# A decoder block on one Trainium2 core: the last gate's weights as one load of 128 rows and one of twelve blocks of eight rows

## The chip, the core and the metric

The kernel runs on one core of a Trainium2 chip. The core has five engines that run their own instruction streams and meet at semaphores: TensorE (PE, matrix products into PSUM), VectorE (DVE), ScalarE (ACT), GpSimd (POOL) and SyncE (SP), which here issues nearly all loads. Loads from HBM into SBUF, whose 128 rows are called partitions, are carried out by 16 DMA engines that work side by side; a load counts as landed when every engine that takes part has finished its share. The metric is the device time of one execution in microseconds (us).

## The reference

It is one block of a transformer for four sequences with one new position each (B = 4, D = 512), with adaptive layer norm from a condition `c`. Cut to what matters:

```python
mod = (silu(c) @ w_mod).reshape(4, 6, 1, 512)
sa, ca, ga, sb, cb, gb = mod[:, 0], ..., mod[:, 5]
h = layernorm(x) * (1 + ca) + sa
x = x + ga * attention(h)          # 32 heads, 8 groups, the last 2048 of 8192 keys and values
h = layernorm(x) * (1 + cb) + sb
x = x + gb * ((silu(h @ w1) * (h @ w3)) @ w2)
```

`w_mod` has 512 rows and 6 x 512 columns. The last gate, `gb`, needs the 512 rows of its last 512 columns: 1 MB of float32.

## The kernel before

All of it is float32 and nearly all of it is loading: 101 MB of weights, keys and values pass through SBUF once. Two buffers, `KV0` and `KV1` (16384 columns of 128 partitions each), take turns for the keys and values of the eight head groups, and `WP` takes attention's projections.

The order of the loads is that of SyncE's instructions, lines 91 to 125, through the helper `load` (lines 88 and 89). Waits on semaphores hold a load back until the buffer that it overwrites is free; lines 95 to 116 are attention's. Behind attention come, in this order: `wm_in` (three of the modulations) and `f1_in` (`w1` and a part of `w3`) into `KV0`, lines 118 and 119; then, once the last group's values have been used, into `KV1`: `f2_in` (the rest of `w3`) in two parts (lines 121 and 122), `gb_in`, the weights of the last gate, on the semaphore `dgb` (line 123), and `w2_in` in six pieces with the semaphores `dw0` to `dw5`, cut at the chunks 0, 4, 8, 10, 12, 13 and 14 of 512 columns (lines 124 and 125, `W2_CUTS`).

At the start, `t0_in` (line 91) brings `c`, arranged as 128 partitions by 16 columns (4 blocks of 128 rows by 4 sequences), and the first two modulations' weights. ScalarE and VectorE make `sc = silu(c)` of it (lines 181 to 188); TensorE multiplies with it from line 312 on.

TensorE's stream has the block `pair` (lines 326 to 352), run four times for two head groups each, `query` and `leave`, and then the feed-forward part in one run. The end of it, which the change touches:

- lines 403 to 440: the products with `w1` and `w3`, silu and the hidden layer `hidT`;
- lines 443 to 446: TensorE waits for `dgb` and multiplies `sc` with the four blocks of 128 rows of the gate's weights. Each block k of four has its own four PSUM rows from 32k on in the bank `bM`;
- line 448: ScalarE copies the whole bank to `gb_sb`;
- lines 452 to 475: the product with `w2`, piece by piece as `dw0` to `dw5` arrive. Behind piece 0, TensorE adds the gate's four partial sums with the matrix `same` (lines 461 to 465), and ScalarE copies them to `gbJ`; behind piece 1, VectorE copies the first sums to `y_sb` (line 471), which TensorE adds behind piece 2 (line 475);
- lines 477 to 482: gate and residual on VectorE, and the store.

`_layout` (line 487) arranges the inputs on the host before the launch. The functions that the diff touches:

Of the kernel before, what the change touches and what calls it, by code (L numbers as in the profile page):

```python
# [5 lines left out]
AF = mybir.ActivationFunctionType  # L6
# [4 lines left out]
B, D, HQ, G, SK, DH, W, FF = 4, 512, 32, 8, 8192, 128, 2048, 1792  # L11
P = 128
# [2 lines left out]
EPS = 1e-5  # L15
CHUNKS = [(j, c) for c in range(4) for j in range(4) if c < 2 or j < 3]
HEAD = 8
W2_CUTS = [0, 4, 8, 10, 12, 13, 14]
PAIRS = G // 2

# [20 lines left out]
        return (self.sem, self.n)  # L41


def block_kernel(nc, x_in, t0_in, t1_in, kv_in, w_in, wm_in, f1_in, f2_in, gb_in, w2_in, out):
    T, v, s, gp, S = nc.tensor, nc.vector, nc.scalar, nc.gpsimd, nc.sync

    def sems(names):
        return [nc.alloc_semaphore(n) for n in names.split()]

    def sb(name, cols, rows=P):  # L50
        return nc.alloc_sbuf_tensor(name, (rows, cols), F32).ap()

    def bank(name):
        return nc.alloc_psum_tensor(name, (P, 512), F32).ap()

    (first,) = sems("first")
    A = Queue(nc, s, "act")
    V = Queue(nc, v, "dve")
    L = Queue(nc, gp, "pool")
    dx, dt0, dt1, dkv, dk, dva, dvb, dwo, dm, df1, df2a, df2b, dgb = sems("dx dt0 dt1 dkv dk dva dvb dwo dm df1 df2a df2b dgb")  # L60
    dw = sems(" ".join(f"dw{i}" for i in range(len(W2_CUTS) - 1)))
    z_ok, q_ok, p_ok, k_ok, va_ok, vb_ok, pt_ok, o_ok, ot_ok = sems("z_ok q_ok p_ok k_ok va_ok vb_ok pt_ok o_ok ot_ok")
# [2 lines left out]

    KV = [sb("KV0", 16384), sb("KV1", 16384)]
    WP = sb("WP", 8192)
    T0 = KV[1][:, : 16 + 4096]
    x_sb = sb("x_sb", 512, B)
    ident, same, eps = sb("ident", P), sb("same", B), sb("eps", 1)  # L70
    sc, e1, e2 = sb("sc", 16), sb("e1", 16), sb("e2", 16)
    hT, h2T = sb("hT", 16), sb("h2T", 16)
    Z = sb("Z", B * 28)
    q_sb, p_sb, o_sb, a_sb, y_sb, g_sb, u_sb, gb_sb = [sb(n, 512) for n in "q_sb p_sb o_sb a_sb y_sb g_sb u_sb gb_sb".split()]
# [10 lines left out]
    bS, bQ, bT, bP, bO, bX, bA, bM = [bank(n) for n in "bS bQ bT bP bO bX bA bM".split()]  # L85


    def load(dst, src, sem):
        S.dma_start(dst, src).then_inc(sem, 16)  # L89

    load(T0, t0_in, dt0)
    s.dma_start(WP[:, 4096:], t1_in).then_inc(dt1, 16)
# [27 lines left out]
    S.wait_ge(o_done, G)  # L120
    load(KV[1][:, :3072], f2_in[:, :3072], df2a)
    load(KV[1][:, 3072:6144], f2_in[:, 3072:], df2b)
    load(KV[1][:, 6144:8192], gb_in, dgb)
    for a, b, sem in zip(W2_CUTS[:-1], W2_CUTS[1:], dw):
        load(KV[1][:, 8192 + a * 512 : 8192 + b * 512], w2_in[:, a * 512 : b * 512], sem)


    l_eps = L.op(gp.memset(eps, EPS))
    t = L.op(gp.memset(ident, 0.0))
# [49 lines left out]
    v_same = V.op(v.tensor_reduce(same, ident.rearrange("p (j i) -> p i j", i=32)[:, :B, :], axis=AX.X, op=ALU.add))  # L179

    A.wait((dt0, 16))
    t = A.op(s.activation(e1, T0[:, :16], AF.Exp, scale=-1.0))
    V.wait(t)
    t = V.op(v.tensor_scalar(e2, e1, 1.0, None, op0=ALU.add))
    V.wait(t)
    t = V.op(v.reciprocal(e2, e2))
    V.wait(t, (dt0, 16))
    t_sc = V.op(v.tensor_mul(sc, T0[:, :16], e2))  # L188

    A.wait((pe, 1))  # L190
    t_sa = A.op(s.copy(sa_sb, bM[32 : 32 + B, :]))
# [1 line left out]
    t = V.op(v.scalar_tensor_tensor(xs, bM[:B, :], 1.0, xc, op0=ALU.add, op1=ALU.mult))  # L193
# [71 lines left out]
    def mm(o, lhsT, rhs, start=True, stop=True):  # L265
        return T.matmul(o, lhsT, rhs, start=start, stop=stop, skip_group_check=True)  # L266
# [45 lines left out]
    T.wait_ge(V.sem, t_sc[1])  # L312
    for k in range(4):
        for i in range(2):
            ins = mm(bM[32 * i : 32 * i + B, :], sc[:, k * B : (k + 1) * B], T0[:, 16 + (2 * k + i) * 512 : 16 + (2 * k + i + 1) * 512], k == 0, k == 3)
    ins.then_inc(pe, 1)
    T.wait_ge(V.sem, t_h[1])
    for k in range(4):
        ins = T.transpose(bT[:, k * B : (k + 1) * B], h[:, k * P : (k + 1) * P], ident[:B, :B])
# [51 lines left out]
    for k in range(4):  # L371
        for i in range(3):
            at = (3 * k + i) * 512
            ins = mm(bX[32 * i : 32 * i + B, :], sc[:, k * B : (k + 1) * B], KV[0][:, at : at + 512], k == 0, k == 3)
# [5 lines left out]
    t = V.op(v.tensor_mul(ag, bM[:B, :], ga_sb))  # L380
# [13 lines left out]
    for k in range(4):  # L394
        ins = T.transpose(bT[:, k * B : (k + 1) * B], h[:, k * P : (k + 1) * P], ident[:B, :B])
# [4 lines left out]
    def view(t_):  # L400
        return t_.rearrange("p (c j i) -> p c j i", c=4, j=4)
# [4 lines left out]
    for k in range(4):  # L406
        for j in range(4):
            at = 6144 + k * 2048 + j * 512
            ins = mm(bQ[32 * j : 32 * j + B, :], h2T[:, k * B : (k + 1) * B], KV[0][:, at : at + 512], k == 0, k == 3)
# [3 lines left out]
    for k in range(4):  # L413
# [5 lines left out]
        for j in range(3):  # L419
            at = k * 1536 + j * 512  # L420
            ins = mm(bA[32 * j : 32 * j + B, :], h2T[:, k * B : (k + 1) * B], KV[1][:, at : at + 512], k == 0, k == 3)
    ins.then_inc(pe, 1)
    A.wait((pe, 7))
    t = A.op(s.activation(view(eT), view(bP)[:, :, :, :B], AF.Exp, scale=-1.0))
    V.wait(t)
    t = V.op(v.tensor_scalar(dT, eT, 1.0, None, op0=ALU.add))
    V.wait(t)
    t = V.op(v.reciprocal(rT, dT))
# [7 lines left out]
    for c in range(4):  # L436
        ins = T.transpose(bS[:, c * P : c * P + 96], u_sb[:96, c * P : (c + 1) * P], ident[:96, :96])
# [2 lines left out]
    t_hid = V.op(v.tensor_mul(view(hidT)[:, :, :3], view(sT)[:, :, :3], view(bS)[:, :, :3, :B]))  # L440


    T.wait_ge(dgb, 16)
    for k in range(4):
        ins = mm(bM[32 * k : 32 * k + B, :], sc[:, k * B : (k + 1) * B], KV[1][:, 6144 + 512 * k : 6144 + 512 * (k + 1)])
    ins.then_inc(pe, 1)
    A.wait((pe, 10))
    t_gb = A.op(s.copy(gb_sb, bM))
    T.wait_ge(V.sem, t_hid[1])
    hw = view(hidT)  # L450
    w2 = KV[1][:, 8192 : 8192 + 14 * 512].rearrange("p (n m) -> p n m", n=14)
    for i in range(len(W2_CUTS) - 1):
        T.wait_ge(dw[i], 16)
        for n in range(W2_CUTS[i], W2_CUTS[i + 1]):
            jj, c = CHUNKS[n]
            if n < HEAD:
                ins = mm(bO[32 * (n % 4) : 32 * (n % 4) + B, :], hw[:, c, jj, :], w2[:, n, :], n < 4, n >= HEAD - 4)
                continue
            for j in range(4):
                ins = mm(bX[32 * j : 32 * j + B, :P], hw[:, c, jj, :], w2[:, n, j * P : (j + 1) * P], n == HEAD, n == 13)  # L460
        if i == 0:
            T.wait_ge(A.sem, t_gb[1])
            for j in range(4):
                ins = mm(bT[32 * j : 32 * j + B, :P], same, gb_sb[:, j * P : (j + 1) * P])
# [13 lines left out]
    t = V.op(v.tensor_mul(yt, bX[:, :P], gbJ))  # L478
# [8 lines left out]
def _layout(i):  # L487
    import numpy as np

    def a(t):  # L490
        return np.ascontiguousarray(t)

    k = i["A_k_cache"][:, :, SK - W :, :].reshape(B, G, NT, 512, DH)
    v = i["A_v_cache"][:, :, SK - W :, :].reshape(B, G, NT, 4, P, DH)
    k = k.transpose(1, 4, 2, 0, 3).reshape(G, P, 8192)
    v = v.transpose(1, 4, 2, 0, 3, 5).reshape(G, P, 8192)
    wm = i["w_mod"].reshape(4, P, 6, 512).transpose(1, 0, 2, 3)
    c = i["c"].reshape(B, 4, P).transpose(2, 1, 0).reshape(P, 16)
    wq = i["A_wq"].reshape(4, P, G, 512).transpose(2, 1, 0, 3).reshape(G, P, 2048)
    wo = i["A_wo"].reshape(G, R, P, D).transpose(0, 2, 1, 3).reshape(G, P, 2048)  # L500
    pairs = [[wo[2 * p], wo[2 * p + 1]] + ([wq[2 * p + 2], wq[2 * p + 3]] if p < 3 else [wo[6], wo[7]]) for p in range(4)]
    w1 = i["B_w1"].reshape(4, P, FF).transpose(1, 0, 2)
    w3 = i["B_w3"].reshape(4, P, FF).transpose(1, 0, 2)
    w2 = i["B_w2"].reshape(14, P, D)
    return {
        "x_in": a(i["A_x"].reshape(B, D)),
        "t0_in": np.concatenate([c, wm[:, :, 1::-1].reshape(P, 4096)], 1),
        "t1_in": np.concatenate([wq[0], wq[1]], 1),
        "kv_in": np.concatenate([k, v], 2),
        "w_in": np.stack([np.concatenate(p, 1) for p in pairs]),  # L510
        "wm_in": a(wm[:, :, 2:5]).reshape(P, 6144),
        "f1_in": np.concatenate([w1, w3[:, :, 1536:]], 2).reshape(P, 8192),
        "f2_in": a(w3[:, :, :1536]).reshape(P, 6144),
        "gb_in": a(wm[:, :, 5]).reshape(P, 2048),
        "w2_in": a(np.stack([w2[4 * j + c_] for j, c_ in CHUNKS], 1)).reshape(P, 14 * D),
    }

# [14 lines left out]
```

## Time and profile before

| | us |
|---|---|
| median of 3 runs | 243.03 (243.0 to 243.1) |
| the profiled execution | 243.09 |
| its span, first to last instruction | 241.7 |
| TensorE busy, matmuls | 137.8 (57% of the span) |
| VectorE busy | 38.6 (16%) |
| ScalarE busy | 25.1 (10%) |
| GpSimd busy | 1.7 (1%) |

The profile is of one execution. Its page gives each engine's busy time, the DMA queues, the chain of work that ended last and the costliest groups of instructions; further views of the same trace give windows of time, waits and single instructions. The 16 DMA engines serve several queues: q1 is SyncE's loads and q10 ScalarE's, while q8 and q14 carry the fetches of the engines' own instructions. The views give what all 16 engines move together, and no view says which engine moved a packet.

### The profile page before, as it was taken

The page shows a single profiled execution, that of the slowest core. Times are in us where ns is not written, and L with a number is a line of the kernel's source. Part 1 is how long each engine was busy: PE and PEld are TensorE (multiplying, and loading weights), DVE is VectorE, ACT ScalarE, POOL GpSimd, SP SyncE. Part 2 cuts the span into 40 slices and gives each one's busy share as a digit, 9 for nine tenths or more (in the row PEclk, how much of TensorE's full clock was granted, in tenths as well). Part 3 has the DMA queues.
Part 4 walks back from the last instruction along what each step waited for, and adds up shares of the span by engine and source line. Part 5 has one row for each costly group of instructions (what it writes and reads, how often), then busy time and mean ns, then how long its engine had stood idle before and what let it go on. Part 6 is the DMA issues. An engine that isn't in the chain of part 4 may idle for free. (4 is left out here: it accounts for less than half of the span.)

```text
span 241.7 us, 2238 instructions
## 1 busy us (share of the span) xinstructions
PE 137.8 (57%) x940; PEld 38.0 (16%) x940; DVE 38.6 (16%) x126; ACT 25.1 (10%) x54; POOL 1.7 (1%) x14
## 2 busy tenths in 40 slices
PE   3004677726771478267713782877137869656964
PEld 0000122201220013112200130121001312111211
DVE  3003203202200022022000220130002222133112
ACT  2002002100010011010100110011002100133110
POOL 2000000000000000000000000000000000000000
PEclk9999959968798579887985898679758997995999
DMA  7998989899989898999898989998989999999993
GB/s 266 440 511 358 510 361 499 369 423 439 504 369 499 369 499 370 423 428 504 369 499 369 499 369 423 434 510 369 499 347 445 442 396 445 449 431 394 413 415 116
DMA packets 4045, 101.34 MB, mean 419 GB/s; under 512 B 452, under 2 KB 580, under 8 KB 1096
## 3 DMA queue, kind: packets, MB, share of 16 engines
q1 hardware_dynamic: 3888, 99.17, 95.7%
q10 hardware_dynamic: 152, 2.11, 2.1%
q8 instruction: 3, 0.05, 0.1%
q14 instruction: 2, 0.02, 0.0%
HBM read 101.20 MB, written 0.07 MB: 419 GB/s over the span
## 5 line engine op out<-in xcount | busy, mean ns | idle before, releaser
L266 PE MATMUL bS<-KV,Z 128*16 128x512 f32 x256 | 42.7, 828 | 39.2 <-PEq L269 39.2
L266 PE MATMUL bO<-KV,pT 128*16 128x512 f32 x256 | 32.5, 652 | 0.5
L266 PEld LDWEIGHTS bS<-KV,Z 128*16 128x16 f32 x256 | 9.3, 123 | 67.1 <-issue 67.1
L222 DVE TENSOR_REDUCE MX<-bS 128x1 f32<-128x512 f32 x8 | 5.5, 692 | 80.4 <-PE bS L266 80.4
L266 PE MATMUL bM<-KV,sc 128*4 128x512 f32 x24 | 6.9, 801 | 16.6 <-DVE sc L188 16.6
L230 ACT ACTIVATE p_sb<-bS,NB 128x512 f32<-128x512 f32 x8 | 5.5, 687 | 101.2 <-DVE NB L228 101.2
L287 PE MATMUL bP<-ident,p_sb 128*128 128x128 f32 x32 | 5.6, 303 | 16.6 <-PEq L269 16.6
L266 PE MATMUL bA<-WP,oT 128*4 128x512 f32 x64 | 11.1, 773 | 4.3 <-PEq L269 4.3
L266 PEld LDWEIGHTS bO<-KV,pT 128*16 128x16 f32 x256 | 8.2, 107 | 23.9 <-issue 23.9
L251 ACT ACTIVATE o_sb<-bO,LB 128x512 f32<-128x512 f32 x8 | 5.5, 687 | 48.8 <-PE bO L266 48.8
L266 PE MATMUL bQ<-WP,hT 128*4 128x512 f32 x64 | 9.2, 647 | 0.6 <-DVE hT L197 0.6
L287 PE MATMUL bX<-ident,o_sb 128*128 128x128 f32 x32 | 5.0, 280 | 7.2 <-PEq L269 7.2
L254 DVE TENSOR_REDUCE oT<-bX 128x16 f32<-128x64 f32 x8 | 1.8, 224 | 43.6 <-PE bX L287 43.6
L287 PEld LDWEIGHTS bP<-ident,p_sb 128*128 128x128 f32 x32 | 3.6, 148 | 24.0 <-issue 24.0
L287 PE MATMUL bT<-ident,q_sb 128*128 128x128 f32 x32 | 5.5, 298 | 3.2 <-PEq L269 3.2
L201 ACT ACTIVATE q_sb<-bQ 128x512 f32<-128x512 f32 x8 | 4.7, 593 | 13.3 <-PE bQ L266 13.3
L287 PEld LDWEIGHTS bX<-ident,o_sb 128*128 128x128 f32 x32 | 3.4, 141 | 14.3 <-issue 14.3
L235 DVE COPY pT<-bP 128x256 f32<-128x256 f32 x8 | 3.4, 424 | 13.5 <-PE bP L287 13.5
L266 PE MATMUL bQ<-KV,h2T 128*4 128x512 f32 x32 | 5.3, 816 | 0.3 <-DVE h2T L398 0.3
L287 PEld LDWEIGHTS bT<-ident,q_sb 128*128 128x128 f32 x32 | 3.6, 150 | 8.0 <-issue 7.7
L266 PEld LDWEIGHTS bM<-KV,sc 128*4 128x4 f32 x24 | 1.0, 104 | 22.4 <-DVE sc L188 18.2
L266 PE MATMUL bX<-KV,sc 128*4 128x512 f32 x24 | 4.2, 592 | 0.0
(100 smaller groups left out, 65.2 us busy)
## 6 DMA issues: line engine op xcount, KB each, us to landing
WP<-w_in SPq DMA_DIRECT2D x3, 4096.0 KB, 22.0
KV<-kv_in SPq DMA_DIRECT2D x1, 4096.0 KB, 24.3
KV<-f_in SPq DMA_DIRECT2D x1, 4096.0 KB, 28.0
KV<-kv_in SPq DMA_DIRECT2D x1, 3072.0 KB, 31.1
KV<-wm_in SPq DMA_DIRECT2D x1, 3072.0 KB, 18.4
KV<-f_in SPq DMA_DIRECT2D x2, 1536.0 KB, 19.2
KV<-t_in SPq DMA_DIRECT2D x1, 2056.0 KB, 12.2
WP<-t_in ACTq DMA_DIRECT2D x1, 2048.0 KB, 12.4
```

What stands on the lines that cost most here:

```text
L201: A.op(s.mul(q_sb, bQ, DH**-0.5), q_ok)
L222: t = V.op(v.reduce_max(MX[:, 0:1], bS, axis=AX.X))
L230: A.op(s.activation(p_sb, bS, AF.Exp, bias=NB[:, 0:1], accum_out=SM[:, 0:1]), p_ok)
L235: v.tensor_copy(pT.rearrange("p (t b c r) -> p c b t r", t=NT, b=B, c=4), bP.rearrange("p (c b i) -> p c b i", c=4, b=B)[:, :, :, :16].rea ...
L251: A.op(s.mul(o_sb, bO, LB[:, 0:1]), o_ok)
L254: V.op(v.tensor_reduce(oT.rearrange("p (r b) -> p r b", r=R), diag, axis=AX.X, op=ALU.add), ot_ok)
L266: return T.matmul(o, lhsT, rhs, start=start, stop=stop, skip_group_check=True)
L287: ins = T.transpose(dst[:, c * P : (c + 1) * P], src[:, c * P : (c + 1) * P], ident)
```

## The change

Nothing of what is computed changes. The 512 columns of the gate's weights are cut at `GA = 320`. For the first 320 columns, the 512 rows are still four blocks of 128. For the other `GB = 192` columns, the first 128 rows are one block, and the other 384 rows are four blocks of 96.

- `gb_in` holds the 128-partition parts, 4 x 320 + 192 = 1472 columns for 2048. A new input `gc_in` holds the four blocks of 96, 768 columns for 96 partitions. On the host it is an array of 12 x 9 x 768, of which eight of nine rows are used, so that the load reads twelve blocks of eight rows with a gap behind each block. Both loads raise `dgb`, and TensorE waits for 32 in place of 16.
- The silu is also taken of `c` arranged as 96 partitions by 16 columns (`c96`, the other partitions zero); `sc`, `e1` and `e2` have 32 columns in place of 16, and `t0_in` brings 16 columns more.
- The gate's four matmuls of 512 columns become four of 320 and five of 192, to the same PSUM rows; the first of the four blocks of 96 is added to the product of the block of 128.
- `w2_in` lies 192 columns further on in `KV1`.

```diff
+GA = 320
+GB = 512 - GA
+W2_AT = 8192 + GB
...
-    T0 = KV[1][:, : 16 + 4096]
+    T0 = KV[1][:, : 32 + 4096]
-    sc, e1, e2 = sb("sc", 16), sb("e1", 16), sb("e2", 16)
+    sc, e1, e2 = sb("sc", 32), sb("e1", 32), sb("e2", 32)
...
-    load(KV[1][:, 6144:8192], gb_in, dgb)
+    load(KV[1][:, 6144 : 6144 + 4 * GA + GB], gb_in, dgb)
+    load(KV[1][:96, 6144 + 4 * GA + GB : 8192 + GB], gc_in[:, :8], dgb)
     for a, b, sem in zip(W2_CUTS[:-1], W2_CUTS[1:], dw):
-        load(KV[1][:, 8192 + a * 512 : 8192 + b * 512], w2_in[:, a * 512 : b * 512], sem)
+        load(KV[1][:, W2_AT + a * 512 : W2_AT + b * 512], w2_in[:, a * 512 : b * 512], sem)
...
-    T.wait_ge(dgb, 16)
-    for k in range(4):
-        ins = mm(bM[32 * k : 32 * k + B, :], sc[:, k * B : (k + 1) * B], KV[1][:, 6144 + 512 * k : 6144 + 512 * (k + 1)])
+    T.wait_ge(dgb, 32)
+    for k in range(4):
+        mm(bM[32 * k : 32 * k + B, :GA], sc[:, k * B : (k + 1) * B], KV[1][:, 6144 + GA * k : 6144 + GA * (k + 1)])
+    mm(bM[:B, GA:], sc[:, :B], KV[1][:, 6144 + 4 * GA : 6144 + 4 * GA + GB], True, False)
+    for k in range(4):
+        at = 6144 + 4 * GA + GB * (k + 1)
+        ins = mm(bM[32 * k : 32 * k + B, GA:], sc[:96, 16 + k * B : 16 + (k + 1) * B], KV[1][:96, at : at + GB], k > 0, True)
     ins.then_inc(pe, 1)
...
+    c96 = np.zeros((P, 16), c.dtype)
+    c96[:96] = i["c"].reshape(B, 512)[:, P:].reshape(B, 4, 96).transpose(2, 1, 0).reshape(96, 16)
+    wg = wm[:, :, 5]
+    gc = np.zeros((12, 9, 4 * GB), wg.dtype)
+    gc[:, :8] = i["w_mod"][P:, 5 * 512 + GA : 6 * 512].reshape(4, 96, GB).transpose(1, 0, 2).reshape(12, 8, 4 * GB)
...
-        "gb_in": a(wm[:, :, 5]).reshape(P, 2048),
+        "gb_in": np.concatenate([a(wg[:, :, :GA]).reshape(P, 4 * GA), wg[:, 0, GA:]], 1),
+        "gc_in": gc,
```

More of the change, by code (lines that the diff above doesn't have):

```diff
@@ L41, in op, with block_kernel @@
         return (self.sem, self.n)
-def block_kernel(nc, x_in, t0_in, t1_in, kv_in, w_in, wm_in, f1_in, f2_in, gb_in, w2_in, out):
+def block_kernel(nc, x_in, t0_in, t1_in, kv_in, w_in, wm_in, f1_in, f2_in, gb_in, gc_in, w2_in, out):
     T, v, s, gp, S = nc.tensor, nc.vector, nc.scalar, nc.gpsimd, nc.sync
@@ L181, in block_kernel @@
     A.wait((dt0, 16))
-    t = A.op(s.activation(e1, T0[:, :16], AF.Exp, scale=-1.0))
+    t = A.op(s.activation(e1, T0[:, :32], AF.Exp, scale=-1.0))
     V.wait(t)
@@ L187, in block_kernel @@
     V.wait(t, (dt0, 16))
-    t_sc = V.op(v.tensor_mul(sc, T0[:, :16], e2))
+    t_sc = V.op(v.tensor_mul(sc, T0[:, :32], e2))
     A.wait((pe, 1))
@@ L314, in block_kernel @@
         for i in range(2):
-            ins = mm(bM[32 * i : 32 * i + B, :], sc[:, k * B : (k + 1) * B], T0[:, 16 + (2 * k + i) * 512 : 16 + (2 * k + i + 1) * 512], k == 0, k == 3)
+            ins = mm(bM[32 * i : 32 * i + B, :], sc[:, k * B : (k + 1) * B], T0[:, 32 + (2 * k + i) * 512 : 32 + (2 * k + i + 1) * 512], k == 0, k == 3)
     ins.then_inc(pe, 1)
@@ L450, in block_kernel @@
     hw = view(hidT)
-    w2 = KV[1][:, 8192 : 8192 + 14 * 512].rearrange("p (n m) -> p n m", n=14)
+    w2 = KV[1][:, W2_AT : W2_AT + 14 * 512].rearrange("p (n m) -> p n m", n=14)
     for i in range(len(W2_CUTS) - 1):
@@ L506, in _layout @@
         "x_in": a(i["A_x"].reshape(B, D)),
-        "t0_in": np.concatenate([c, wm[:, :, 1::-1].reshape(P, 4096)], 1),
+        "t0_in": np.concatenate([c, c96, wm[:, :, 1::-1].reshape(P, 4096)], 1),
         "t1_in": np.concatenate([wq[0], wq[1]], 1),
```

## The prediction

> **What bounds the kernel now.** I read the page first: the busy shares, the DMA rows, and the chain that ended last.
>
> ```profile
> span 241.7 us, 2238 instructions
> q1 hardware_dynamic: 3888, 99.17, 95.7%
> q8 instruction: 3, 0.05, 0.1%
> q14 instruction: 2, 0.02, 0.0%
> DMA 12%; PE 3%; SPq 1%; DVE 0%; issue 0%
> ```
>
> Queue q1, SyncE's loads, fills the 16 DMA engines for 95.7% of the span. The chain names DMA with only 12%, because it stops at the instruction that issued the last load; in order of time, the same chain ends so:
>
> ```profile
> 210.14 28.79 DMA KV<-w_in
> 238.97 0.45 PE bX L266 x8
> 239.44 0.30 DVE yt L478
> 239.77 0.29 DVE y L480
> ```
>
> The last piece of `w2_in` is issued at 210.14 and lands at 238.93 (210.14 + 28.79); behind it come one group of matmuls, two VectorE operations and the store. A load is done when the last of the 16 engines has done its share, so I asked for tenths of a microsecond at the end (busy time of each engine, granted clock, DMA share, GB/s):
>
> ```profile
> core 0: us, PE busy (x) PEld busy (x) DVE busy (x) ACT busy (x) POOL busy (x), PEclk, DMA share, GB/s
> 237.00:237.10 0.10, 0.10 (x8) 0.08 (x8) 0.00 (x0) 0.00 (x0) 0.00 (x0) 1.00 0.44 164
> ...
> 237.40:237.50 0.10, 0.02 (x4) 0.00 (x0) 0.00 (x0) 0.00 (x0) 0.00 (x0) 1.00 0.21 82
> ...
> 237.70:237.80 0.10, 0.09 (x4) 0.09 (x8) 0.00 (x0) 0.00 (x0) 0.00 (x0) 1.00 0.21 82
> 237.80:237.90 0.10, 0.10 (x8) 0.10 (x9) 0.00 (x0) 0.00 (x0) 0.00 (x0) 1.00 0.17 62
> 237.90:238.00 0.10, 0.10 (x12) 0.10 (x8) 0.00 (x0) 0.00 (x0) 0.00 (x0) 1.00 0.10 41
> ...
> 238.20:238.30 0.10, 0.10 (x8) 0.00 (x0) 0.00 (x0) 0.00 (x0) 0.00 (x0) 1.00 0.11 41
> 238.30:238.40 0.10, 0.07 (x8) 0.04 (x8) 0.00 (x0) 0.00 (x0) 0.00 (x0) 1.00 0.05 20
> 238.40:238.50 0.10, 0.10 (x8) 0.07 (x8) 0.00 (x0) 0.00 (x0) 0.00 (x0) 1.00 0.05 20
> 238.50:238.60 0.10, 0.10 (x8) 0.00 (x0) 0.00 (x0) 0.00 (x0) 0.00 (x0) 1.00 0.01 0
> ```
>
> This is a staircase. At the end one engine moves about 20 GB/s, so 82 GB/s are four engines, 62 three, 41 two. Twelve engines have stopped by about 237.4; the other four stop at about 237.55, 237.9, 238.3 and 238.5. **The load ends 1.1 us later than its twelve early engines**, and that tail is the whole margin here: perfectly spread, lags of 0.15, 0.5, 0.9 and 1.1 us would cost each engine 2.65/16 = 0.17 us, and the end would come 0.9 us sooner.
>
> Where do four lags come from? The DMA view of four short stretches, 33.5 to 35, 91.5 to 93, 206 to 207.5 and 213 to 215 us, shows in each one instruction fetch:
>
> ```profile
> q8 instruction: 1, 0.02, 4.3%
> q14 instruction: 1, 0.01, 1.4%
> q14 instruction: 1, 0.01, 1.3%
> q8 instruction: 1, 0.02, 3.4%
> ```
>
> Four fetches, two of about 16 KB and two of about 8 KB, and four late engines, two late by about 1 us and two by half of it or less. I read it so that each fetch pushed one engine back and, as the queue never runs dry, it stayed behind.
>
> **The change part by part.** *The moved bytes.* From the DMA view (load, KB, us from issue to landing):
>
> ```profile
> KV<-gb_in SPq DMA_DIRECT2D x1, 1024.0 KB, 22.8
> KV<-w_in SPq DMA_DIRECT2D x2, 256.0 KB, 28.7
> ```
>
> The load of `gb_in` (1024 KB, 64 KB for each engine if sixteen share it) becomes one of 128 rows of 1472 columns (736 KB, 46 KB each) and one of twelve blocks of eight rows of 768 columns (288 KB). No transfer of before has an outer size of twelve, so its spread is unknown: from all sixteen engines (nothing shifts) to twelve (24 KB each, and nothing for four). I take twelve, one block each, as rows go to engines whole in the equal shares of every other load. Then four engines lose 18 KB and twelve gain 6 KB. The rate of one engine:
>
> ```profile
> 231.00:233.00 2.00, 1.74 (x16) 0.60 (x20) 0.20 (x1) 0.42 (x1) 0.00 (x0) 1.00 0.98 408
> 235.50:236.00 0.50, 0.50 (x8) 0.00 (x0) 0.00 (x0) 0.00 (x0) 0.00 (x0) 1.00 0.96 369
> ```
>
> 408/(0.98 x 16) = 26.0 GB/s with rows of 8 KB, 369/(0.96 x 16) = 24.0 with the 2 and 4 KB rows of the last pieces. Rows of 5.75 KB I take at 25.7 and of 3 KB at 24: a relieved engine needs 47.1/25.7 = 1.83 us in place of 65.5/26.0 = 2.52, **-0.69 us**; another 1.83 + 24.6/24 = 2.85, **+0.33 us** (6.1/26 = +0.24 if smaller rows cost nothing; I take +0.30). All pieces of `w2_in` come behind this load on every engine, so both shifts reach the end.
>
> [...]
>
> *Which four are relieved* decides, and no view names a packet's engine. With all four late ones relieved, the end is max(238.5 - 0.69, 237.4 + 0.30) = 237.81: -0.69 us. With the two latest but not the third, it is 237.9 + 0.30 = 238.2: -0.30. With only the latest, 238.3 + 0.30 = 238.6: +0.1. With the latest not among them, 238.8: +0.30. I take the second: the two latest fit the two larger fetches of queue q8, so one origin, the lesser two those of q14; a rule that puts one pair on high engines need not hold for the other.
>
> *What follows the load.* The three late steps of TensorE and what they wait for:
>
> ```profile
> 231.47 1.04 PE L266 MATMUL bM<-KV,sc 128*4 128x512 f32 x8
> 232.77 1.04 PE L266 MATMUL bO<-KV,hidT 128*4 128x512 f32 x8 [0.26 <-DMA KV<-w_in]
> 235.16 1.04 PE L266 MATMUL bO<-KV,hidT 128*4 128x512 f32 x8 [1.14 <-DMA KV<-w_in]
> ```
>
> The gate's four matmuls (eight instructions, 1.04 us) become nine: 4 x 320 + 5 x 192 = 2240 columns for 2048, so +0.10 us by columns, and at most 1.04 x 10/8 = 1.30 if each of the ten added instructions takes as long as one of before. I take 0.10, as the columns are what these eight instructions spend their time on. It hides in the 0.26 us and then the 1.14 us that TensorE waits for `w2_in`, 1.40 together; ScalarE's copy of the gate (line 448) moves with it and is used before the second wait. With pieces 0.30 us earlier 1.10 of the cover is left, so the upper end would give 0.2 of the gain back; with no cover it would cost its whole 0.1 to 1.3. The wait for both loads (32 for 16) stands where the old one stood; behind it are only matmuls that need later loads. Once the second piece is in, every step waits for a piece, and all pieces shift alike.
>
> *Issue.* SyncE issues one load more, ahead of the pieces of `w2_in`:
>
> ```profile
> 207.29 0.43 SPq L89 DMA_DIRECT2D KV<-gb_in  x1
> 207.77 12.21 SPq L89 DMA_DIRECT2D KV<-w_in  x6
> ```
>
> +0.47 us of issue (the distance of these two rows, 207.29 to 207.77) for pieces that land some 20 us and more after their issue. The last issue already stands until 219.98 (207.77 + 12.21); one load more in the queue may hold it for another load's time (line 122's 1.57 MB at 408 GB/s, 3.9 us), still 13 us ahead of the end. It costs nothing; on an empty queue it would cost 0.47.
>
> *Start.* `t0_in` grows by 64 bytes for each row, 8 KB over all; four operations (lines 182 to 188) work on 32 columns for 16. What hides the latter is that the loads run through meanwhile:
>
> ```profile
> 12.00:31.00 19.00, 7.59 (x28) 1.31 (x28) 3.98 (x13) 1.99 (x6) 0.00 (x0) 0.95 1.02 443
> ```
>
> At 443 GB/s the 8 KB are 0.02 us on every engine; a pause of the loads would let the operations' few hundredths count too.
>
> Sum: -0.30 + 0.02 = **-0.28 us**. The profiled execution took 243.09 us, 1.39 beyond its span; the median of the three runs is 243.03. So 243.03 - 0.28 = **242.75 us**, -0.12%. Measurements of this kernel can tell about 0.2% (0.49 us) from no change, so this counts as the same.
>
> **The rivals.** *All four are relieved:* -0.69 + 0.02, 242.36 us (-0.28%), faster. For it: four late, four relieved. Against it: two kinds of fetch, and nothing ties both to the same engines.
>
> *The late ones are not relieved, or the load spreads over sixteen:* +0.1 to +0.3 us, 243.1 to 243.35, and 243.1 where the change doesn't shift anything and only smaller rows are paid for. For it: four of sixteen are relieved, so a given engine has one chance in four if nothing guides the choice.
>
> *Slower: two engines write to one place.* In loads of 128 rows each engine writes eight rows; if twelve blocks of eight neighbouring rows put two engines on one entrance to SBUF, both go at half rate, and 24.6 KB take 2.05 us for 1.02, +1.0 us on these. The price counts from the point where such an engine's stop passes 238.5: an early one ends at 237.4 + 0.30 + 1.0 = 238.7, +0.2 us, 243.25; the third latest at 237.9 + 1.3 = 239.2, +0.7 us, 243.75; the latest at 239.8, +1.3, 244.35. Against it: every load of before keeps 24 to 26 GB/s for each engine, so no sharing has been seen; for it: none of them has blocks of eight neighbours.
>
> [...]
>
> **How the numbers follow.** Forecast (two latest relieved, 242.75) 0.35; all four (242.36) 0.22; not the late ones or no shift (243.1 to 243.35) 0.25; sharing 0.18, a third of it under 243.6. The range 242.2 to 243.6 leaves out the dearer sharing, 0.12, and a little at its lower end. Faster by over 0.2%: most of the second case and the better edge of the first, 0.25. Slower: the dearer sharing and the edge of the third, 0.19. Within: 0.56.
>
> **What would show each step.** The tenths of a microsecond at the end: stops of two engines only past the rest, the last near 238.2, would bear the forecast out; no tail and an end near 237.8, the second case; a tail up to 238.8, the third. Sharing shows as a DMA share near 1 with less than 380 GB/s from about 226 to 230. TensorE's waits for `w2_in` must stay, the 0.26 us excepted. What could upset it: the last of the page's three q8 fetches falls past 236.5, where most engines are done. If the added instructions of TensorE draw it forward onto a busy engine, it makes a fifth late one.

## The result and the profile after

| | before | after |
|---|---|---|
| median of 5 runs | 243.03 us (243.0 to 243.17) | 244.95 us (244.33 to 245.37) |
| profiled execution | 243.09 us | 244.33 us |
| its span | 241.7 us | 242.9 us |

The ratio is 1.0072 [1.0053, 1.0092]: slower by 0.7%, where 242.75 us was forecast. The kernel is as full of loads as it was. From the page of after (span, the loads' queue, the shares of the chain that ended last):

```profile
span 242.9 us, 2259 instructions
...
q1 hardware_dynamic: 3996, 99.17, 95.7%
...
DMA 8%; SPq 5%; PE 3%; DVE 0%; issue 0%
```

The end has the same form too. The chain of after in order of time (start, duration, what):

```profile
219.65 20.50 DMA KV<-w_in
240.14 0.04 issue
240.18 0.45 PE bX L270 x8
240.63 0.02 issue
240.65 0.30 DVE yt L486
240.96 0.02 issue
240.98 0.29 DVE y L488
```

Matmuls, VectorE and store behind the last piece take what they took before (0.45, 0.30 and 0.29 us). The piece lands at 240.14 in place of 238.93: +1.21 us, and the span grew by 1.2. So what was lost was lost ahead of that landing. Where, the windows of after show (busy time of the engines, granted clock, DMA share, GB/s):

```profile
226.00:227.00 1.00, 1.00 (x12) 0.19 (x7) 0.00 (x0) 0.00 (x0) 0.00 (x0) 1.00 1.01 421
227.00:228.00 1.00, 1.00 (x13) 0.29 (x9) 0.00 (x0) 0.59 (x1) 0.00 (x0) 1.00 1.06 387
228.00:229.00 1.00, 1.00 (x11) 0.18 (x3) 0.00 (x0) 0.00 (x0) 0.00 (x0) 1.00 1.15 255
229.00:230.00 1.00, 1.00 (x10) 0.45 (x12) 0.20 (x1) 0.22 (x1) 0.00 (x0) 1.00 0.94 279
230.00:231.00 1.00, 1.00 (x12) 0.10 (x3) 0.93 (x3) 0.00 (x0) 0.00 (x0) 1.00 0.96 329
231.00:232.00 1.00, 0.30 (x3) 0.00 (x0) 0.65 (x2) 0.00 (x0) 0.00 (x0) 1.00 0.99 410
```

and, for the three microseconds from 228, after and before in one row each:

```profile
228.00:231.00 3.00, 3.00 (x25) 0.73 (x16) 1.12 (x4) 0.22 (x1) 0.00 (x0) 1.00 1.02 288
```

```profile
228.00:231.00 3.00, 2.20 (x17) 0.45 (x15) 1.82 (x5) 0.22 (x1) 0.00 (x0) 1.00 1.02 426
```

Read the last two columns together. The DMA share is 1.02 in both, so no engine ran dry; yet 288 GB/s went through in place of 426. **Busy engines that move a third less take longer over each transfer**; the 3 KB packets of `gc_in` took 182 ns in the mean, those of e2 below 124. 3 x (426 - 288)/426 = 0.97 us of loading went there, most of the 1.21. A DMA share near 1 with less than 380 GB/s is the sign that the prediction named for sharing.

The tail itself, in tenths of a microsecond of after, is not longer than before:

```profile
238.20:238.30 0.10, 0.10 (x8) 0.08 (x8) 0.00 (x0) 0.00 (x0) 0.00 (x0) 1.00 0.75 287
...
238.90:239.00 0.10, 0.08 (x4) 0.08 (x8) 0.00 (x0) 0.00 (x0) 0.00 (x0) 1.00 0.21 82
239.00:239.10 0.10, 0.10 (x8) 0.10 (x11) 0.00 (x0) 0.00 (x0) 0.00 (x0) 1.00 0.12 41
239.10:239.20 0.10, 0.10 (x12) 0.10 (x8) 0.00 (x0) 0.00 (x0) 0.00 (x0) 1.00 0.11 41
239.20:239.30 0.10, 0.10 (x14) 0.05 (x4) 0.00 (x0) 0.00 (x0) 0.00 (x0) 1.00 0.05 20
...
239.60:239.70 0.10, 0.10 (x8) 0.05 (x8) 0.00 (x0) 0.00 (x0) 0.00 (x0) 1.00 0.01 0
```

Two engines (41 GB/s) run past 239.0 and one (20 GB/s) to about 239.6. But the others, done by 237.4 before, now stop between about 238 and 239: the whole group moved back.

One thing does not fit into this profile. The median lies 1.92 us above before, the profiled execution only 1.24. The five runs are 244.33 and 244.38, then 244.95, 245.08 and 245.37; the profile shows one of the lower pair. The upper ones come back below.

### The profile page after: what moved, and what is told of

Read it like the earlier page. It is cut to its first block, busy times and chain, and to the rows that moved or that the text cites. A ratio compares the mean times of both kernels' runs of the same rounds, so it can differ in the third digit from the quotient of the medians.

```text
span 242.9 us, 2259 instructions
## 1 busy us (share of the span) xinstructions
PE 135.6 (56%) x950; PEld 37.9 (16%) x950; DVE 38.8 (16%) x126; ACT 25.1 (10%) x54; POOL 1.7 (1%) x14
## 3 DMA queue, kind: packets, MB, share of 16 engines
q1 hardware_dynamic: 3996, 99.17, 95.7%
## 5 line engine op out<-in xcount | busy, mean ns | idle before, releaser
L270 PE MATMUL bS<-KV,Z 128*16 128x512 f32 x256 | 43.6, 843 | 44.0 <-PEq L273 44.0
L270 PE MATMUL bM<-KV,sc 128*4 128x512 f32 (+3 forms) x34 | 6.5, 576 | 16.6 <-DVE sc L192 16.6
L270 PE MATMUL bA<-WP,oT 128*4 128x512 f32 x64 | 9.4, 661 | 3.5 <-PEq L273 3.5
L270 PE MATMUL bQ<-WP,hT 128*4 128x512 f32 x64 | 8.3, 592 | 0.6 <-DVE hT L201 0.6
L270 PEld LDWEIGHTS bM<-KV,sc 128*4 128x4 f32 (+1 forms) x34 | 1.3, 93 | 22.2 <-DVE sc L192 18.1
```

## The experiments

The theories, by the letters that the expectations use: **S**, two engines that write to one place in SBUF at a time slow each other (the author's hypothesis; its half rate is an assumption). **N**, nothing is shared, and the cost comes from the smaller rows, the extra issue or TensorE's added instructions.

**Blocks of eight rows alone.** The kernel before, with its 1 MB of `gb_in` read as sixteen blocks of eight rows; bytes, matmuls and waits are those of before:

```diff
-    load(KV[1][:, 6144:8192], gb_in, dgb)
+    load(KV[1][:, 6144:8192], gb_in[:, :8], dgb)   # gb_in: 16 x 9 x 2048
```

> The kernel before, whose one load of the gate's weights (128 rows, 1 MB) is read as sixteen blocks of eight rows with a gap in the source: the same bytes, rows and instructions, all sixteen engines alike. Theory S (eight neighbouring rows for each engine make two engines write to one place at a time, at half rate): the 65.5 KB of an engine take 5.0 us in place of 2.5, so about 245.5 us. Theory N (sharing has nothing to do with it; the change is slow for its smaller rows, its twelve engines or its instructions): 243.0 to 243.1. [...]

247.85 us (247.34 to 248.0), ratio 1.0192 [1.0179, 1.0205]. The direction is S's and the size twice what S gave. One row over nine microseconds of this kernel:

```profile
226.00:235.00 9.00, 5.85 (x44) 1.56 (x36) 2.02 (x6) 0.81 (x2) 0.00 (x0) 1.00 0.99 230
```

The kernel before, in the five microseconds from 226:

```profile
226.00:231.00 5.00, 3.94 (x29) 0.92 (x23) 1.82 (x5) 0.62 (x2) 0.00 (x0) 1.00 1.01 420
```

All engines busy (0.99) at 230 GB/s: against 420 that is 9 x (420 - 230)/420 = 4.1 us of the 4.8. The block form alone costs time, with the issue, the number of engines and the instructions of before; N falls for this part.

**The rest of the change alone.** The kernel before, `gb_in` cut into two loads of 128 rows (5 KB and 3 KB rows) and eight matmuls:

```diff
-    load(KV[1][:, 6144:8192], gb_in, dgb)
+    load(KV[1][:, 6144:7424], gb_in[:, :1280], dgb)
+    load(KV[1][:, 7424:8192], gb_in[:, 1280:], dgb)
...
-    T.wait_ge(dgb, 16)
+    T.wait_ge(dgb, 32)
```

> The kernel before with the gate's weights in two loads of 128 rows (320 and 192 columns of each block) and eight matmuls for four: one issue more, rows of 5 and 3 KB and more TensorE instructions as in the change, but no blocks and no shift between engines. S: 243.1 (0.1 us for smaller rows). N, if the issue, the rows or the instructions cost: 243.6 or more.

243.15 us, 1.0004 [0.9995, 1.0013]. The extra issue, the 3 KB rows, the second wait and four added matmuls together cost nothing that can be measured.

**Ninety-six rows without the gap.** The changed kernel, with `gc_in` a plain array of 96 x 768 (six rows for each engine, if all sixteen take an equal share):

```diff
-    load(KV[1][:96, 6144 + 4 * GA + GB : 8192 + GB], gc_in[:, :8], dgb)
+    load(KV[1][:96, 6144 + 4 * GA + GB : 8192 + GB], gc_in, dgb)
```

> The changed kernel, whose 96 rows are read without the gap, as 96 rows in a line: six rows for each of sixteen engines if they are spread so; all else as in the change. [...] N, if twelve engines are the cost: 243.1.

244.46 us (244.2 to 244.55), 1.0056 [1.0043, 1.0069]; 1.4 us above N's 243.1. Its four slow microseconds:

```profile
227.00:231.00 4.00, 3.87 (x28) 0.91 (x22) 1.21 (x5) 0.62 (x2) 0.00 (x0) 1.00 1.05 293
```

4 x (420 - 293)/420 = 1.2 us. So the loss does not need the gap behind each block: 96 plain rows have it too. How many engines took them is not shown.

**Another shape at another place.** The changed kernel, the same bytes, but as twelve blocks of four rows of 6 KB on the partitions 32 to 79; the gate's other 384 rows are eight blocks of 48, padded with zeros in `sc` (48 columns), and make eight matmuls:

```diff
-    load(KV[1][:96, 6144 + 4 * GA + GB : 8192 + GB], gc_in[:, :8], dgb)
+    load(KV[1][32:80, 6144 + 4 * GA + GB : W2_AT], gc_in[:, :4], dgb)   # gc_in: 12 x 5 x 1536
```

> The changed kernel with the moved part as twelve blocks of four rows of 6 KB on the rows 32 to 79 in place of eight rows of 3 KB on 0 to 95; the same bytes for each of the twelve engines, the contraction in eight blocks of 48 rows (four matmuls more). [...] N: as the change, 244.3 to 245.4. [...]

243.31 us (242.63 to 243.64, 12 runs), 1.0009 [1.0, 1.0017]. The loss is gone: 1.6 us less than after. The median is not the 242.75 of the forecast, but the profiled execution is near it: 242.66 us, its last piece down at 238.46 by the chain, 0.47 us sooner than before:

```profile
215.31 23.16 DMA KV<-w_in
238.46 0.04 issue
238.51 0.45 PE bX L270 x8
```

Beside its views, the trace records when each engine raises a load's semaphore. From the end of `f2_in` to the first piece of `w2_in`, in order of lateness, the two latest engines need 4.29 us for 4.96 in before, and the third latest 5.25 for 4.96: -0.67 and +0.29, the prediction's -0.69 and +0.30. Without the loss, the terms held in this execution.

**The same blocks, 32 partitions lower down.** To leave only one difference, e4 with the partitions 0 to 47 for 32 to 79:

```diff
-    load(KV[1][32:80, 6144 + 4 * GA + GB : W2_AT], gc_in[:, :4], dgb)
+    load(KV[1][:48, 6144 + 4 * GA + GB : W2_AT], gc_in[:, :4], dgb)
```

> e4_rows4 with one thing changed: the twelve blocks of four rows lie on the rows 0 to 47 in place of 32 to 79. [...] N (four rows of 6 KB are simply a better shape than eight of 3 KB): as e4, 242.6 to 243.6.

244.76 us (243.59 to 245.25), 1.0073 [1.0058, 1.0087]. Bytes, blocks, row sizes and instructions are those of e4; only the partition numbers differ. Two microseconds of this kernel (e10), then the same two of e4:

```profile
228.00:230.00 2.00, 2.00 (x16) 0.67 (x16) 1.00 (x4) 0.22 (x1) 0.00 (x0) 1.00 0.94 249
```

```profile
228.00:230.00 2.00, 2.00 (x16) 0.63 (x13) 0.26 (x2) 0.22 (x1) 0.00 (x0) 1.00 1.07 443
```

249 GB/s for 443, 2 x (443 - 249)/443 = 0.9 us; by the chain of e10 the last piece lands at 239.39 (215.31 + 24.08) for e4's 238.46, +0.93:

```profile
215.31 24.08 DMA KV<-w_in
```

**What the pair shows**: the place in SBUF, not the shape of the load, costs the time (0.93 us at the last landing), as S would have it and N would not. Nor are the low partitions slow by themselves: e11 and e12 below load blocks of four rows on 0 to 31 and lose nothing like it (243.16 and 243.30 us). That the cause is two engines at one place remains the author's account: no record has an engine's number, and the pair does not tell apart whether the blocks hold up each other or also the neighbouring loads of 128 rows.

The trace also keeps a record of each packet (size, start, duration). It shows the same at the level of one row (mean duration of a packet, ns):

| packets | in kernels without the loss | in kernels with it |
|---|---|---|
| 3 KB, `gc_in` or its like | 124 (e2) | 182 (after) |
| 6 KB, `gc_in` | 238, all within 234 to 246 (e4) | 356, up to 479 (e10) |
| 8 KB, late loads | 313, up to 324 (before) | 336, up to 679 (after); 345, up to 798 (e3) |
| 12 KB, `f2_in` | 464, up to 473 (before) | 483, up to 1358 (e1) |

The last two lines are a likely reason why S's price was too low in e1: packets of the neighbouring loads of 128 rows, which in before show no such delay, were held up as well.

**The two groups.** The runs of e4 are 242.63 and 242.66, and ten from 243.17 to 243.64. What parts them? **K**: TensorE is late in some executions, as its waits are nearly used up; **V**: which engines are late, and by how much, varies from one execution to the next. In e4, the wait ahead of the second piece is gone, and the gate's matmuls took 1.51 us for 1.04:

```profile
232.51 1.51 PE L270 MATMUL bM<-KV,sc 128*4 128x320 f32 x25
```

So four kernels with the gate's matmuls ahead of the transposes of `u_sb`, where TensorE otherwise waits 0.8 us for VectorE: e6 is e4 so changed, e7 the same with 128 columns for 192 moved, e8 is the changed kernel, e9 the kernel before.

```diff
+    T.wait_ge(dgb, 32)
...
     T.wait_ge(V.sem, t_u[1])
     for c in range(4):
         ins = T.transpose(bS[:, c * P : c * P + 96], u_sb[:96, c * P : (c + 1) * P], ident[:96, :96])
```

> e4_rows4 with TensorE's gate matmuls (and the copy behind them) ahead of the four transposes of u_sb, in the 0.80 us that TensorE waits there, in place of behind them. Theory K (in e4 the loads come early enough that TensorE, whose waits of 0.26 and 1.14 us for the first two pieces are gone there, is late in most runs): 242.65 in all runs, as in the profiled run of e4. Rival V (the runs of e4 differ by which DMA engines the instruction fetches push back, and TensorE has no part in it): as e4, 242.6 to 243.6 with a median near 243.3.

> e6_rows4_early with 128 columns in the moved part in place of 192: by the terms of the prediction the four engines lose 0.46 us and the twelve gain 0.20. The third latest of the profile of before (0.5 to 0.6 us ahead of the last) then ends 0.1 us earlier than with 192 columns and the two latest still ahead of it: 242.55 to 242.7. If the relieved two were the last again: 242.7 to 242.8. V: spread as e4.

> The changed kernel with the gate's matmuls in the same earlier place. S (two engines write to one place): 244.3 to 245.4, as the change, since the loads set the end. If TensorE's longer gate were what the change costs: below 243.9.

> The kernel before with the gate's matmuls in the same earlier place: 243.0 to 243.1, no change, as TensorE waits for the pieces there. A gain of over 0.2 us would mean that TensorE was on the path of before already.

| | median (range) | ratio | runs |
|---|---|---|---|
| e6 | 243.09 (242.62 to 243.5) | 1.0004 [0.9996, 1.0013] | five of 242.62 to 242.83, 242.99, six of 243.19 to 243.5 |
| e7 | 243.31 (242.71 to 243.43) | 1.0009 [1.0, 1.0018] | 242.71, 242.75, 243.04, eight of 243.24 to 243.43 |
| e8 | 244.75 (243.6 to 244.93) | 1.0066 [1.0052, 1.0081] | 243.6, 243.71, four of 244.66 to 244.93 |
| e9 | 243.07 (242.85 to 243.27) | 1.0002 [0.9993, 1.0011] | one group |

The groups stay with TensorE's work out of the way: K falls. That e9 gains nothing shows besides that TensorE was not on the path before, and e8's median, far above 243.9, that TensorE's longer gate is not what the change costs. V is left, but no profile shows an upper run: all seven profiled executions of kernels with two groups (after, e4, e6, e7, e8, e10, e11) lie in the lower one, where only about a third of their 64 runs are. Whether being profiled has to do with it was not tested.

**Are the groups tied to the engines that the load takes?** The expectations call two accounts of it M1 and M2: the engine that is latest in the upper group is one of the eight that e11's load leaves out (M1), or one of the eight that it takes (M2). e11 has eight blocks of four rows on the partitions 0 to 31 (96 columns moved, matmuls early), so that eight engines are relieved if each block takes one, as the twelve blocks of after took twelve:

```diff
+    load(KV[1][:32, 6144 + 4 * GA + GB : W2_AT], gc_in[:, :4], dgb)   # GA = 416; gc_in: 8 x 5 x 1152
```

> e6_rows4_early with eight blocks of four rows on the rows 0 to 31 in place of twelve, and 96 columns in place of 192: eight engines gain 0.35 us, eight lose 0.35. The runs of the kernels that relieve four engines lie in two groups some 0.65 us apart (e4: 242.65 and 243.2 to 243.6), and every profiled run was in the lower one. Theory M1: in the upper group the latest engine is not one of the four relieved, but one of the other four of the upper half; then all runs here lie together near 242.75. M2: it is among the lower eight: two groups, near 242.75 and 243.4. If the groups have nothing to do with late engines (TensorE, the store, the start), they stay 0.65 us apart with the lower at 242.75 too; M2 and this are not told apart by this run.

243.16 us (12 runs), 1.0001 [0.9992, 1.001]: five runs of 242.45 to 242.89 and seven of 243.13 to 243.41. The groups remain; M1 falls.

The last four add to the kernel before a load that nobody reads, so that the engines it takes get more to do and nothing is relieved: eight blocks of four rows of 3 KB (e12), four such blocks (e13), and both with rows of 6 KB (e14, e15):

```diff
     load(KV[1][:, 6144:8192], gb_in, dgb)
+    load(KV[0][:32, 14336:15104], gc_in[:, :4], dgb)   # e13, e15: KV[0][:16]; e14, e15: 14336:15872
...
-    T.wait_ge(dgb, 16)
+    T.wait_ge(dgb, 32)
```

> The kernel before with a load more behind the gate's: eight blocks of four rows (3 KB each, rows 0 to 31) that nothing reads, so that eight engines do 12 KB more, 0.46 us, and nobody is relieved. If in a part of the executions one of these eight is among the latest (M2): two groups, the lower near 243.1, the upper near 243.5 (243.03 + 0.46). If never: 243.0 to 243.2 in all runs, as the two latest of the profile, in the other engines, set the end. If the two groups of the earlier kernels come of something else: 243.0 to 243.2 too.

> [...]

> e12_add8 with twice the bytes: eight engines do 24 KB more, 0.92 us. In the profiles the third latest engine is about 0.6 us ahead of the last, and it is among these eight, so that alone gives +0.3: 243.3, give or take 0.2, in all runs. M2 (in a part of the executions one of these eight is as late as the latest): a second group near 243.95 (243.03 + 0.92).

> [...]

| | added to each engine taken (one to a block) | median (range) | ratio |
|---|---|---|---|
| e12, eight blocks | 12 KB | 243.30 (242.91 to 243.71) | 1.0008 [0.9999, 1.0017] |
| e13, four | 12 KB | 243.03 (242.81 to 243.28) | 0.9999 [0.999, 1.0008] |
| e14, eight | 24 KB | 243.25 (243.03 to 244.26) | 1.0011 [1.0002, 1.0021] |
| e15, four | 24 KB | 243.25 (243.12 to 243.39) | 1.0006 [0.9997, 1.0016] |

24 KB are about 1.0 us of one engine (24.6 KB at 24 GB/s) and show as 0.2 us in e14 and in e15, near the 0.3 expected if the third latest engine, some 0.6 us ahead of the last, is one of those taken. The group near 243.95 us that M2 asked for is not there: of e14's eleven runs one is at 244.26, the others at 243.03 to 243.54, where a share like that of e11's upper group (seven of twelve) would give six. The spread of e12 decides nothing by itself. M2 is not borne out. Clear groups are seen only where a load takes bytes off some engines. **Why there are two groups stays open.** No version beat both kernels: e4, e6 and e11 are level with before.

## Why the prediction was wrong, step by step

**The step that failed** is the price of the twelve engines under "the moved bytes": +0.30 us, from 24.6 KB at the 24 GB/s of one engine in before's last loads (369 GB/s at a share of 0.96). By the semaphore records, the engines' median moved back by 1.18 us between the end of `f2_in` and the first piece of `w2_in`. In e4, with the same bytes on 32 to 79, it moved by 0.24; the other 0.9 us is what the prediction called sharing, which stood among the rivals with a chance of 0.18. It was discounted because every load of before keeps 24 to 26 GB/s for each engine. But no load of before has blocks of eight neighbouring rows, as the rival itself said: rows that can't show an effect were counted against it.

Point by point:

- *Loads bound the kernel, and the last landing sets the end*: right. Queue q1 has 95.7% again, and span and landing grew by the same 1.2 us.
- *Twelve engines*: right. In the semaphore records of after, the two loads raise `dgb` from 16 and from 12 engines as they land. No record has an engine's number, so which twelve these are, and whether any of the late ones are "high", is not shown.
- *The two latest engines relieved, the third latest not*: right, though it was one choice among four on thin evidence. In the packet records of after, the two latest engines end their 5.75 KB rows at 230.04 and 230.21 us and go on with 8 KB rows at once, while a single series of 3 KB rows still runs, the third latest engine's, until 230.63. That engine lands last, 1.28 us behind the median engine. As the twelve were slowed by so much more, the relief could not show. It shows in e4, 242.66 us in the profiled execution for the forecast 242.75, though not in e4's median of 243.31.
- *Each fetch pushes one engine back*: right, as far as order in time can show it. In before, one engine falls 1.31 us behind the median between the loads that land at 32 and 51 us (fetch of q8 at 33.9), a second 0.86 between 80 and 100 us (q14 at 92.0), a third 0.51 between 202 and 209 us (q14 at 206.6), and a fourth by 219 us (q8 at 213.4), when the two of q8 are 1.26 and 1.47 behind. They stay so to the end.
- *The rival's price*, 24.6 KB in 2.05 us for 1.02, +1.0 us: near in size for the engines' median (0.9), too small where whole neighbouring loads are held up (4.1 us in e1 for 64 KB an engine, where halving the rate gives 2.5). For the third latest engine the rival gave 1.3 us with the bytes and 243.75 us; that engine lost 1.53 us, and the profiled execution has 244.33. The half rate behind the price was the author's assumption; in the mean, packets took about half as long again (3 KB 182 ns for 124, 6 KB 356 for 238).
- *TensorE*: hidden, as forecast, but by less room than thought. The gate took 1.35 us for 1.04, 0.31 more where 0.10 was chosen, and above the upper end of 1.30; the first wait, 0.26, is gone and the second keeps its 1.14. In after (start, duration, line, matmul, wait):

```profile
232.59 1.35 PE L270 MATMUL bM<-KV,sc 128*4 128x320 f32 x18
233.97 1.04 PE L270 MATMUL bO<-KV,hidT 128*4 128x512 f32 x8
...
236.37 1.04 PE L270 MATMUL bO<-KV,hidT 128*4 128x512 f32 x8 [1.14 <-DMA KV<-w_in]
```

- *Issue*: +0.47 was too low, and still hidden. The issue of `gc_in` took 0.94 us, and the pieces behind it start at 209.72, 1.95 later than before's 207.77 (0.99 of it from `gc_in`, the rest ahead of it); the last piece was still issued 20.5 us ahead of its landing. e2 shows an added issue to cost nothing. SyncE's own timeline in after:

```profile
208.26 0.43 SPq L92 DMA_DIRECT2D KV<-gb_in  x1
208.73 0.94 SPq L92 DMA_DIRECT2D KV<-gc_in  x1
209.72 13.11 SPq L92 DMA_DIRECT2D KV<-w_in  x6
```

- *Start*, +0.02 us: too small to be seen. e4 makes `t0_in` 16 columns wider still and is level with before.
- *The third fetch of q8 might move forward*: it did not; it falls between 236 and 238 us in both.

**What is accounted for.** In the profile the last piece lands 1.21 us later. The engine that lands last in after is the third latest ahead of the new load; in before, the third latest landed 0.63 us ahead of the last (238.30 for 238.93). In after it was 0.33 us later already at the end of `f2_in` (227.34 for 227.01), and from there to the first piece it took 6.49 us for 4.96: -0.63 + 0.33 + 1.53 gives the 1.2. Of the 1.53, 0.29 is the bytes, as in e4, and 1.2 is the loss that e4 does not have. The 0.33 is a difference between executions: e8, with the same loads, has 226.85 at that place and ends 0.73 us sooner. Of the median's +1.92, the other 0.68 is that most runs of after lie in the upper group. No run explains that part.

## What to carry to other kernels

When a load has its own block shape, time it at two places in SBUF before its bytes are priced at the rate of the other loads: in the profiles, the same bytes took 0.9 us less on partitions 32 to 79 than on 0 to 47. A DMA share near 1 with fewer GB/s than in the neighbouring windows was the sign of it here (1.02 at 288 GB/s, for 426 in before), and the share alone hides it. When a risk can't be seen in any row of the kernel before, that the rows look well is no evidence against it.

## What the runs showed of the hardware

- In the kernels with the loss, packets of the neighbouring loads were slow as well: 8 KB packets took up to 679 ns in after, for a mean of 313 before, and 12 KB packets of `f2_in` up to 1358 ns in e1, for 464. With sixteen blocks of eight rows the core moved 230 GB/s for nine microseconds.
- In before, one engine fell behind the others around each of the four instruction fetches at 33.9, 92.0, 206.6 and 213.4 us, and stayed so: the two of 16 KB (33.9 and 213.4) took 1.03 and 1.10 us, and behind the second two engines were 1.26 and 1.47 us later than the median. The third latest engine was 0.59 to 1.02 us behind at the end of `f2_in`, by the execution (all profiles but e1's).
- Ninety-six plain rows lost as well (e3): 293 GB/s over four microseconds, +1.4 us, though the load has no gap.
- The kernels here in which a load takes bytes off some engines have runs in two groups, 0.6 to 0.8 us apart in e4, e6, e7, e11 and after, 1.1 to 1.2 in e8 and e10. Of the others, e2, e3, e9, e13 and e15 stay within 0.5 us each, e1 and e12 spread over 0.7 and 0.8, and e14 has one run 0.7 us above its others.
- In e1, TensorE was granted half its clock while the late loads still came, and eight matmuls that took 1.04 us before took 1.89. From the windows and the chain of e1:

```profile
238.00:239.00 1.00, 1.00 (x8) 0.15 (x4) 0.00 (x0) 0.00 (x0) 0.00 (x0) 0.50 1.03 414
```

```profile
239.92 1.89 PE bO L266 x8
241.81 2.35 PE bX L266 x56
244.15 0.02 issue
244.17 0.30 DVE yt L478
```

  The chain names TensorE, but this cost nothing that can be seen. By the semaphore records the last piece landed at 243.66 us, 4.73 later than before, and VectorE began 0.51 us behind it, as before (238.93 and 239.44). The loads account for nearly all of e1's 4.8 us. Why the clock was lower was not taken apart.
